# Write order of permuted copies, list lengths and a new pick string in an attention and Fourier-mixing kernel

## The chip, the core and the metric

The kernel runs on one core of a Trainium2 chip. A core has a matrix engine (TensorE, PE in the profile), a vector engine (VectorE, DVE), a scalar engine (ScalarE, ACT), a general engine (GpSimd, POOL) and a queue engine (SyncE, SP), which here issues nearly all transfers. Each engine works off its own queue in order, and engines wait for one another through semaphores. Matrix products and transposes land in PSUM, which has eight banks; the other engines copy the results to SBUF, the working memory. The metric is the device time of one launch in microseconds (us).

## The reference

What is computed, cut to what matters (B = 8, H = 8, S = 576, D = 64, 128 features, model width 512, hidden width 2048, all float32):

```
def phi(x):                        # x = q or k, times 1/sqrt(sqrt(D))
    h = x @ omega.T - sum(x*x)/2
    h = h - max(h, axis=-1)
    return exp(h) / sqrt(128)
q_p, k_p = phi(q), phi(k)
kv  = einsum('bhsm,bhsd->bhmd', k_p, v);   z = sum(k_p, axis=2)
x   = (q_p @ kv) / (q_p @ z + 1e-6)        # heads joined: (B, S, 512)
u   = x + real(fft(fft(x, axis=1), axis=2))
un  = layernorm(u)
out = u + relu(un @ w_ch1) @ w_ch2
```

## The kernel before

The program has two parts, and each is written out from a list. A step (`Step`) names its engine (or two engines to choose from), an assumed length in us, the buffers and PSUM banks that it takes and gives back, and the events that it waits for. `Listing.run` takes one step after another from many streams and emits its instructions; the position in the list is the position in the engine's queue. In the second part, the step that could begin first by the assumed lengths and biases comes next. In the first part, a string `PICKS` (line 63) says for every step which stream goes on and, with a capital letter, that the second-best engine takes it. There the assumed lengths no longer choose the stream, but they still set which of two engines counts as the best, and which bank is taken.

**First part.** Three interleaved streams work through the 32 head pairs (8 batches, 4 pairs each). For one pair (`attn`):

- `loads` and `load_v` issue k, q (tile `kq`, two buffers) and v (`vd`) on SP.
- PE transposes the nine k and q blocks (line 511), ACT copies them out (`kqT`, L521).
- PE projects them on omega (L595), DVE takes the maxima (`nmx`, L539), ACT the exponentials (`e`, L556).
- PE forms kv (L629), and DVE or ACT copies it (`keep`, L643 or L645).
- PE transposes the nine query feature blocks (line 511) in three groups of 1, 4 and 4 blocks (j0 = 0, 1, 5). ACT copies each group from PSUM to `qeT`, permuting the tokens (`evicted`, L530), with two instructions for each group, one for each half of the tokens.
- PE multiplies with kv (L676, L684), DVE forms the reciprocal (L693, L694), and DVE or ACT scales the result to `x` (L705 or L701).

When a batch has its four pairs, `mix` does the Fourier transform: folds on DVE and POOL (L732 to L768), products (L788 to L849), copies (L811, L882), sums (L887 to L900); the rows go to DRAM (`us`, L914, L869, L925). Beside this, `weights` loads 32 blocks of the feed-forward weights as 64-bit floats (`raw`, L468) and `narrow` turns them into float32 on ACT, POOL and DVE (L436 to L454). `plain` runs the feed-forward network for the first 512 rows (L1034, L1057). `norm_of` (line 955) normalises 128 rows: statistics on DVE (L964 to L966), a power on POOL (L968), scaling on DVE (L970), transposes on PE (L974), a copy on ACT (L978).

**Second part.** The remaining 4096 rows go through the feed-forward network in eight blocks of 512 (L1241 and L1421 are its products), with `norm_of` for the next block woven in (`late_norms`). It has no pick string. `norm_of` gets its tile pool as an argument: `mlpp` in the first part, `late` in the second.

In `evicted`, the destination of a group is permuted over (h, s, t, c): c is the block inside the group, and h, t and s split the 128 tokens of a block. c is the fastest in memory. A group of four blocks (h = 4, s = 2, t = 16, c = 4) with j0 = 5 is written with t innermost, in steps of four elements (16 bytes). With j0 = 1 the same shape is written with c innermost, in memory order. The group with j0 = 0 has a single block (c = 1).

Of the kernel before, what the change touches and what calls it, by code (L numbers as in the profile page):

```python
# [14 lines left out]
AF = mybir.ActivationFunctionType  # L15
# [20 lines left out]
PE, ACT, DVE, POOL, SP, NONE = "pe", "act", "dve", "pool", "sp", "none"  # L36
# [3 lines left out]
class Clock(NamedTuple):  # L40
# [20 lines left out]


PICKS = (
    "ff40d00d3cacfgdbgce3gbbcecccegc8cbabfhg0iiii8ef9a89h827edhOiicfhedidjhggciee7ebhJhceadafaedafffbbffb"
    "bfacdceadjccjbhceecfbQcdbd877gjiih7ai7a77gcahKb8b8hgg79h8ehgjeecScjgicejddhhh8b9dgbgbjahdeddaffefcaj"
    "dcgbfgadhidgcf77hb7fefOI7hh1hg96ghif7ge7fQffhdfhfefgch77h8gddTbbjjHe8jfjj8d6k6ddkejmeegjiidhjhfgbhhd"
    "jefjifajkdljajggggNlkfkk7ajjhkdagieLML76m6lknjaa9aecnogaoooe8en8dlllm9cddJcbjj87ccQd9jhljiiildkhgmki"
    "ilghjhjhkfjThfgiQhjikgkhfiie7abj9il07j64758i85j56ijThilgf5dmbdkkegef6hggdc5hcbjibggakdmgbjeaj8l5k9am"
    "3da9hddRah7hjkak4j7j6dlihjfklmcd7jhhjfbef6Ijcemkkkjm6hjh7jgqkgmUdclD9icRicdemielhjjildmchj9milgjFoc9"
    "687nabdeke8ckbHWK7ffgjdi8cjdThfgfhfcklb4aclbjOjaaacca48iahf5Tacfdijefa759bbfbcg8g7aa7feg9b54Q67fdfie"  # L70
    "ggehe5lcdekRRfhccfhjiifkIeecjfickTdeegegebhh86efja9ajffkSagh5eghd9efg9fbddh9cjghjccdkicKccdbfdfhcKeK"
    "f9efdcbdhRc565fifih8fdM9L675SicjRiPPheh7hbhfdj5ggihiIfchfeajgohhdLeN756g8ik7jiibcaJicTajgihji96ha8fj"
    "dkgh7efieh4dch5caafejcdfh5cice9heeeghhbjcgggghlgmkjkcljdioablhmka8aiGI444ompdjh9dmd77ikc9mhngnjjjljk"
    "knminilmkimklknlllTioQJGfgihkagee8h7Whlmkl79h3ld7rlil98cbeg9Lnp9rqqln9mpnabq9dg8s6ejfqk8dYlg8WShcnom"
    "piddpgjijlpkpEfkpeppedphphcncom5mlebkjmjle76646dl5dRecbkimg36mm488kncmiMdMNi5L4fflek966clcdgndkRgei8"
    "gaiaUhjgeklkmml4immb0U0k8k9fjjfjhd2g6ki8m4ljagebdc9agb2hbcfihgddgge9ahPcchdaRhcQhhi8cjcecgLGff6fd9Qa"
    "88a2f7bf8g9R998gb9aM7b9ddbdd35472759eaef9bbfbbcbce9abec666f6g87hd8M7bdcLb6HfgcOKc24f9f79c888Qd8a8e48"
    "eb6bghdeeeca7c877cdcb54e8d4788Jcb4cccfe5ge9I9dKb9b8ec8dded8aadMfe1geg97e59g375f6hdaF8OidNeiahhdbi2hh"
    "cc4hfifjhgfgfihg2gR4ehcS4fjj8gUcaeifcjjggj4bg8ddMf52i46ghhaacb65caKdNdNb3643a891442a6792364755bb76bF"
    "9a8bbb8accd4857bd87d7MaccbLDbbEaL9ccIa249c9a9dbc27eeN9ce8O765e588af73ab979de876aee1fcgdi9SichSa5a5f5"  # L80
    "5e145446cc9GM5ccabc7JaI553958888359012964432bcdb56Nb78b78daca58c78a7187676c56978b0e6510G1bF8a9a77486"
    "75992847bD6F333a77909K929aaFFF5CC66566666622241021110"
)


# [195 lines left out]
def kernel(  # L281
# [10 lines left out]
    nc = tc.nc  # L292
# [54 lines left out]
    mlpp = early.enter_context(tc.tile_pool(name="mlp", bufs=2))  # L347
# [7 lines left out]
    def psum_of(b):  # L355

        i = b.ids[0]
        return banks[:, i] if len(b.ids) == 1 else banks[:, i : i + 2]

    def got():  # L360

        return listing.got, psum_of(listing.got)
# [150 lines left out]
        return dst  # L513

    def evicted(dst, b, j0, j1, makes, order):
        cost = 0.01 + 0.222 * (j1 - j0) if order else 0.05 + 0.107 * (j1 - j0)
        yield Step(ACT, cost, 0.02, makes=makes + (j0,), give=(b,), bias=0.08)
        ps = psum_of(b)[:, 0 : 128 * (j1 - j0)].rearrange("q (c p) -> q c p", p=128)
        dst = dst[:, j0:j1, :]
        if order is None:  # L520
            nc.scalar.activation(out=dst, in_=ps, func=AF.Copy)  # L521
            return
        h, s, t = order[j0]
        dst = dst.rearrange("q c p -> q (c p)").rearrange("q (h s t c) -> q s c h t", h=h, s=s, t=t)
        ps = ps.rearrange("q c (h t s) -> q s c h t", h=h, s=s)
        for i in range(s):
            of, to = ps[:, i, ::-1, :, ::-1] if i and j0 else ps[:, i], dst[:, i]
            if j0 == 1:
                of, to = (a.rearrange("q c h t -> q h t c") for a in (of, to))
            nc.scalar.activation(out=to, in_=of, func=AF.Copy)  # L530

    def softmax(n, ts, num, b, es):

# [183 lines left out]
    def mix(b):  # L717
# [7 lines left out]
        def folds(n):  # L725
            op = (ALU.add, ALU.subtract)[n]
            even, odd = (ALU.subtract, ALU.add) if n else (ALU.add, ALU.subtract)
            step = Step({DVE: 1.135, POOL: 2.45}, take=("half",), port=True)
            yield step
            eng = nc.gpsimd if step.eng == POOL else nc.vector  # L730
            h = fft.tile([P, NC3 + 1, DM], F32, name="half", tag="half")
            eng.tensor_tensor(out=h[:, 0:NL], in0=x[:, 0:NL], in1=x[:, NL : 2 * NL], op=op)  # L732
            yield Step(DVE, 1.0, port=True, bias=-0.08)
            nc.vector.tensor_copy(
                out=h[:, NL, 0 : 2 * QD + 1 : 2 * QD], in_=x[:, 4, 0 : 2 * QD + 1 : 2 * QD]
            )
            for dst, src in ((h[:, 0:NL], h[:, 0:NL]), (h[:, NL : NL + 1], x[:, 4:5])):
                nc.vector.tensor_tensor(
                    out=dst[:, :, 1 : 2 * QD],
                    in0=src[:, :, 1 : 2 * QD],  # L740
                    in1=src[:, :, DM - 1 : 2 * QD : -1],
                    op=op,
                )
            step = Step({DVE: 0.91, POOL: 1.55}, port=True)
            yield step
            eng = nc.gpsimd if step.eng == POOL else nc.vector
            for dst, o in ((NC3, ALU.add), (1, ALU.subtract)):
                eng.tensor_tensor(
                    out=h[:, dst, 0 : 2 * QD + 1],
                    in0=h[:, 0, 0 : 2 * QD + 1],  # L750
                    in1=h[:, 1, 0 : 2 * QD + 1],
                    op=o,
                )
            step = Step(
                {DVE: 1.2, POOL: 2.2},
                makes=("fold", b, n), give=("half",), port=True, bias=-1.41,
            )
            yield step
            eng = nc.gpsimd if step.eng == POOL else nc.vector
            for m, o in ((0, even), (1, odd)):  # L760
                eng.tensor_tensor(
                    out=fold[:, :, 2 * n + m, :],
                    in0=h[:, 1 : NC3 + 1, 0:QD],
                    in1=h[:, 1 : NC3 + 1, 2 * QD : QD : -1],
                    op=o,
                )
            middle = fold[:, :, 3, 0:1] if n else mid_t[:]
            eng.tensor_copy(out=middle, in_=h[:, 1 : NC3 + 1, QD : QD + 1])  # L768
# [5 lines left out]
        for n, (tab, name) in enumerate(((cs, "cs"), (sn, "sn"))):  # L774
# [4 lines left out]
                take=("duo",) + (("y",) if n == 0 else ()),  # L779
# [40 lines left out]
        for c in range(NC3):  # L820
# [6 lines left out]
                take=("duo",),  # L827
# [30 lines left out]
            order = ((1, 0), (1, 1), (0, 0), (0, 1)) if c < NL else ((1, 0), (0, 0), (1, 1), (0, 1))  # L858
# [77 lines left out]
    def load_rows(dst, t):  # L936
        nc.sync.dma_start(dst, us[P * t : P * (t + 1), :])
# [17 lines left out]
    def norm_of(j, t, i, pool, dst):  # L955

        yield Step(SP, 0.42, 3.0, take=("u",), kb=256)
        u = pool.tile([P, DM], F32, name="u", tag="u", bufs=2)
        load_rows(u[:], t)
        st = small.tile([P, 6], F32, name="st", tag="st")  # L960
        mv = small.tile([P, 2], F32, name="mv", tag="mv")
        rstd = small.tile([P, 1], F32, name="rstd", tag="rstd")
        yield Step(DVE, 1.12, bias=-0.23)
        nc.vector.bn_stats(out=st[:], in_=u[:])  # L964
        nc.vector.bn_aggr(out=mv[:], in_=st[:])
        nc.vector.tensor_scalar(rstd[:], mv[:, 1:2], 1e-6, None, op0=ALU.add)  # L966
        yield Step(POOL, 1.05, port=True, bias=-0.18)
        nc.gpsimd.tensor_tensor(rstd[:], rstd[:], mhalf[:], op=ALU.pow)  # L968
        yield Step(DVE, 0.455, port=True)
        nc.vector.tensor_scalar(u[:], u[:], mv[:, 0:1], rstd[:], op0=ALU.subtract, op1=ALU.mult)  # L970
        yield Step(PE, 0.437, take=("bank",), give=("u",))
        b, tp = got()
        for dc in range(NDC):
            nc.tensor.transpose(  # L974
                tp[:, 128 * dc : 128 * dc + 128], u[:, 128 * dc : 128 * dc + 128], ident[:]
            )
        yield Step(ACT, 0.5, give=(b,), makes=("unT", j, i), bias=0.33)
        nc.scalar.activation(  # L978
            out=dst,
            in_=tp.rearrange("p (d t) -> p d t", d=NDC),  # L980
            func=AF.Copy,
        )
# [576 lines left out]
```

## Time and profile before

| | us |
|---|---|
| median of 3 runs (lowest, highest) | 1189.73 (1189.64, 1195.36) |
| the profiled execution | 1192.05 |
| its span, first to last instruction | 1190.2 |
| first product of the second part | 428.6 |

| engine | busy us | share of the span | instructions |
|---|---|---|---|
| PE (matmul) | 1166.4 | 98% | 12765 |
| DVE | 689.0 | 58% | 1482 |
| ACT | 484.1 | 41% | 1602 |
| POOL | 457.2 | 38% | 506 |

The chain of work that ended last, followed back from the last instruction, lies 87% on PE, 4% on ACT, 4% on DVE and 2% on DMA. Rows of the groups that the change names:

| line, engine | what | count | mean ns |
|---|---|---|---|
| L530 ACT | `qeT` from PSUM, 128x256 | 128 | 599 |
| L530 ACT | `qeT` from PSUM, 128x64 | 64 | 314 |
| L732 POOL | `half` from x, 128x1024 | 9 | 2368 |
| L732 DVE | `half` from x, 128x1024 | 7 | 1237 |
| L964, L965, L966 DVE | statistics | 36 each | 684, 182, 154 |
| L968 POOL | the power | 36 | 832 |

A mean over instructions that follow each other closely counts their overlap twice: the time that such an instruction holds its engine is read from one start to the next. Matmul rows overlap in the same way, and a matmul that waits for its operands inside its row counts as busy.

### The profile page before, as it was taken

The page shows a single profiled execution, that of the slowest core. Times are in us where ns is not written, and L with a number is a line of the kernel's source. Part 1 is how long each engine was busy: PE and PEld are TensorE (multiplying, and loading weights), DVE is VectorE, ACT ScalarE, POOL GpSimd, SP SyncE. Part 2 cuts the span into 40 slices and gives each one's busy share as a digit, 9 for nine tenths or more (in the row PEclk, how much of TensorE's full clock was granted, in tenths as well). Part 3 has the DMA queues.
Part 4 walks back from the last instruction along what each step waited for, and adds up shares of the span by engine and source line. Part 5 has one row for each costly group of instructions (what it writes and reads, how often), then busy time and mean ns, then how long its engine had stood idle before and what let it go on. Part 6 is the DMA issues. An engine that isn't in the chain of part 4 may idle for free.

```text
span 1190.2 us, 31894 instructions
## 1 busy us (share of the span) xinstructions
PE 1166.4 (98%) x12765; PEld 1043.5 (88%) x12765; DVE 689.0 (58%) x1482; ACT 484.1 (41%) x1602; POOL 457.2 (38%) x506
## 2 busy tenths in 40 slices
PE   8899999999999999999999999999999999999998
PEld 7778788879787878998998998999999899899898
DVE  5889899986565541752562572464374275256245
ACT  7889899878555212222222222222222222222211
POOL 2455554355354324315314324333332431531521
PEclk9999999999999999999999999999999999999999
DMA  9656856566475260852672573384194185177255
GB/s 260 171 171 183 250 148 210 164 199 190 140 229 167 76 211 10 276 188 69 227 234 80 163 263 115 111 287 143 52 302 131 66 290 179 63 238 222 80 162 193
DMA packets 144708, 205.71 MB, mean 173 GB/s; under 512 B 49072, under 2 KB 58544, under 8 KB 144560
## 3 DMA queue, kind: packets, MB, share of 16 engines
q1 hardware_dynamic: 144064, 203.41, 54.2%
q8 instruction: 101, 1.65, 0.6%
q14 instruction: 47, 0.39, 0.1%
q10 hardware_dynamic: 496, 0.26, 0.1%
HBM read 171.90 MB, written 35.91 MB: 175 GB/s over the span
## 4 chain that ended last, share of the span: by engine, by line
PE 87%; ACT 4%; DVE 4%; DMA 2%; issue 1%; SPq 1%; POOL 0%; DVEq 0%; ACTq 0%; POOLq 0%
PE banks L1241 33%; PE banks L1421 29%; PE banks L1034 5%; PE banks L1057 4%; PE banks L595 4%; PE banks L511 4%; ACT e L556 3%; PE banks L629 2%; PE banks L676 2%; PE banks L838 1%; PE banks L788 1%; DMA kq<-in_q_dram 1%; PE banks L974 1%; DVE nmx L539 1%; DMA raw<-in_moe_w_ch_dram 1%
## 5 line engine op out<-in xcount | busy, mean ns | idle before, releaser
L1421 PE MATMUL banks<-wl,sums 128*128 128x128 f32 x1792 | 219.6, 275 | 0.4
L1421 PEld LDWEIGHTS banks<-wl,sums 128*128 128x128 f32 x1792 | 210.5, 192 | 2.2 <-issue 1.5
L1227 DVE CUSTOM_DVE_ANT_0 hid<-banks,s 128x256 f32<-128x256 f32 x192 | 78.4, 422 | 224.6 <-PE banks L1241 219.8
L1255 ACT ACTIVATE s<-banks 128x256 f32<-128x256 f32 x192 | 73.8, 384 | 247.3 <-PE banks L1241 243.9
L556 ACT ACTIVATE e<-banks,nmx 128x128 f32<-128x128 f32 x576 | 165.1, 447 | 17.8 <-DVE nmx L539 17.2
L1241 PE MATMUL banks<-unT,w 128*128 128x256 f32 x704 | 168.6, 379 | 0.0
L1241 PEld LDWEIGHTS banks<-unT,w 128*128 128x128 f32 x704 | 132.2, 190 | 17.5 <-issue 0.5
L1396 ACT ACTIVATE s<-banks 128x128 f32<-128x128 f32 x168 | 46.6, 278 | 247.1 <-PE banks L1421 192.5
L1401 DVE TENSOR_TENSOR part<-banks,s 128x128 f32<-128x128 f32 x168 | 48.7, 290 | 138.1 <-PE banks L1421 137.9
L1241 PE MATMUL banks<-tt,w1s 128*128 128x256 f32 x512 | 125.0, 379 | 0.0
L1308 POOL TENSOR_TENSOR hs<-hid 128x256 f32<-128x256 f32 x64 | 46.6, 728 | 192.3 <-DVE hid L1227 166.8
L1241 PEld LDWEIGHTS banks<-tt,w1s 128*128 128x128 f32 x512 | 97.2, 190 | 13.3
L539 DVE TENSOR_REDUCE nmx<-banks 128x8 f32<-128x1024 f32 (+1 forms) x96 | 89.3, 951 | 24.8 <-PE banks L595 22.3
L1421 PE MATMUL banks<-wl,hid 128*128 128x128 f32 x768 | 98.8, 275 | 0.0
L1421 PEld LDWEIGHTS banks<-wl,hid 128*128 128x128 f32 x768 | 94.0, 192 | 1.2
L595 PE MATMUL banks<-om,kqT 64*64 64x128 f32 x2304 | 79.1, 274 | 4.4 <-ACT kv L645 1.6
L1308 POOL TENSOR_TENSOR hs<-hid,hs 128x256 f32<-128x256 f32 x64 | 46.6, 728 | 90.2 <-issue 69.6
L1241 PE MATMUL banks<-unT,w1s 128*128 128x256 f32 x320 | 79.5, 379 | 0.0
L968 POOL TENSOR_TENSOR rstd<-rstd,mhalf 128x1 f32<-128x1 f32 x36 | 29.9, 832 | 128.7 <-DVE rstd L966 128.7
L595 PEld LDWEIGHTS banks<-om,kqT 64*64 64x64 f32 x2304 | 63.3, 133 | 15.2 <-issue 4.6
L1421 PE MATMUL banks<-wl,hs 128*128 128x128 f32 x576 | 74.2, 276 | 0.4 <-DVE part L1401 0.4
L530 ACT ACTIVATE qeT<-banks 128x256 f32<-128x256 f32 (+1 forms) x192 | 69.3, 504 | 7.2 <-PE banks L511 6.9
(128 smaller groups left out, 2002.1 us busy)
## 6 DMA issues: line engine op xcount, KB each, us to landing
wl<-w2l SPq DMA_DIRECT2D x392, 256.0 KB, 3.7
raw<-in_moe_w_ch_dram SPq DMA_DIRECT2D x32, 512.0 KB, 5.2
kq<-in_k_dram SPq DMA_DIRECT2D x32, 288.0 KB, 4.5
vd<-in_v_dram SPq DMA_DIRECT2D x32, 288.0 KB, 4.3
kq<-in_q_dram SPq DMA_DIRECT2D x32, 288.0 KB, 4.6
u<-us SPq DMA_DIRECT2D x36, 256.0 KB, 3.7
ur<-us SPq DMA_DIRECT2D x36, 256.0 KB, 4.0
out_dram<-ur SPq DMA_DIRECT2D x34, 256.0 KB, 2.4
```

The source lines that it names most:

```text
L511: nc.tensor.transpose(ps[:, (j - j0) * 128 : (j - j0 + 1) * 128], src(j), ident[:])
L530: nc.scalar.activation(out=to, in_=of, func=AF.Copy)
L539: nc.vector.tensor_reduce(nmx[:, :, 0:num], pps[:, :, 0 : MF * num].rearrange("p b (c m) -> p b c m", m=MF), axis=AX.X, op=ALU.max, negate ...
L556: nc.scalar.activation(out=e[:, c + (i if num == 1 else 0), :], in_=pps[:, i, MF * c : MF * c + MF], func=AF.Exp, bias=nmx[:, i, c : c + 1],)
L595: nc.tensor.matmul(pps[cols, c, MF * m : MF * m + MF], lhsT=kqT[rows, j, cols], rhs=om2[rows, :],)
L1034: nc.tensor.matmul(hp[:, 0:TP], lhsT=w1[:, dc, 128 * fc : 128 * fc + 128], rhs=unTs[key][:, dc, :], start=(dc == 0), stop=(dc == NDC - 1),)
L1227: nc.vector._custom_dve(TENSOR_ADD_SAT, out=o, in0=ps, in1=sb, s0=FMAX, s1=0.0)
L1241: nc.tensor.matmul(ps[:, 0:HT], lhsT=left(dc), rhs=right(dc), start=start and dc == 0, stop=(dc == D2 - 1), skip_group_check=True,)
L1255: nc.scalar.activation(out=s[:], in_=ps[:, 0:HT], func=AF.Copy)
L1308: nc.gpsimd.tensor_tensor(out=o, in0=l, in1=r, op=op)
L1401: nc.vector.tensor_tensor(out=part[:, t, 128 * m : 128 * m + 128], in0=ps[:, 0:128], in1=saved[with_][:], op=ALU.add,)
L1421: nc.tensor.matmul(ps[:, 0:128], lhsT=left[:, f], rhs=wls[j, i, n][:, f], start=start and f == 0, stop=(f == 3), skip_group_check=True,)
```

## The change

The copies of a group are written with c innermost for every group, not only for j0 = 1. The assumed length of such a copy pair changes from 0.01 + 0.222 m to 0.13 + 0.1 m for m blocks. The fold on POOL gets 2.75 for 2.45. The statistics and the power keep 1.12 and 1.05 in the first part and get 1.01 and 0.85 in the second. The pick string of the first part is another one of the same length, 1853 characters; it is said to come from a new search with later transfers.

```diff
 PICKS = (
-    "ff40d00d3cacfgdbgce3gbbcecccegc8cbabfhg0iiii8ef9a89h827edhOiicfhedidjhggciee7ebhJhceadafaedafffbbffb"
...
+    "40e0f03eafdaegebg3bdbbeefccdcccfce8affgg0hhig8ib2La887efjjgeeejjHhighifdjgijdlhhefTfkkefeifhbdfiefhi"
...
     def evicted(dst, b, j0, j1, makes, order):
-        cost = 0.01 + 0.222 * (j1 - j0) if order else 0.05 + 0.107 * (j1 - j0)
+        cost = (0.13 + 0.1 * (j1 - j0)) if order else 0.05 + 0.107 * (j1 - j0)
...
         h, s, t = order[j0]
-        dst = dst.rearrange("q c p -> q (c p)").rearrange("q (h s t c) -> q s c h t", h=h, s=s, t=t)
-        ps = ps.rearrange("q c (h t s) -> q s c h t", h=h, s=s)
+        dst = dst.rearrange("q c p -> q (c p)").rearrange("q (h s t c) -> q s h t c", h=h, s=s, t=t)
+        ps = ps.rearrange("q c (h t s) -> q s h t c", h=h, s=s)
         for i in range(s):
-            of, to = ps[:, i, ::-1, :, ::-1] if i and j0 else ps[:, i], dst[:, i]
-            if j0 == 1:
-                of, to = (a.rearrange("q c h t -> q h t c") for a in (of, to))
-            nc.scalar.activation(out=to, in_=of, func=AF.Copy)
+            of = ps[:, i, :, ::-1, ::-1] if i and j0 else ps[:, i]
+            nc.scalar.activation(out=dst[:, i], in_=of, func=AF.Copy)
...
-            step = Step({DVE: 1.135, POOL: 2.45}, take=("half",), port=True)
+            step = Step({DVE: 1.135, POOL: 2.75}, take=("half",), port=True)
...
-        yield Step(DVE, 1.12, bias=-0.23)
+        yield Step(DVE, 1.12 if pool is mlpp else 1.01, bias=-0.23)
...
-        yield Step(POOL, 1.05, port=True, bias=-0.18)
+        yield Step(POOL, 1.05 if pool is mlpp else 0.85, port=True, bias=-0.18)
```

More of the change, by code (lines that the diff above doesn't have):

```diff
@@ L63 @@
 PICKS = (
-    "ff40d00d3cacfgdbgce3gbbcecccegc8cbabfhg0iiii8ef9a89h827edhOiicfhedidjhggciee7ebhJhceadafaedafffbbffb"
[L65 to L82, printed above, removed]
+    "40e0f03eafdaegebg3bdbbeefccdcccfce8affgg0hhig8ib2La887efjjgeeejjHhighifdjgijdlhhefTfkkefeifhbdfiefhi"
+    "hfjgfkd9elelkjdheefdefQRLbce9h77gh7ijg8cbi877ggk7fihjmngeed87TdecedhIa7g9gg99ieeccdHcdggbhfcgfebbaci"
@@ new lines @@
+    "ebccebRfiedaeecf98g7fI7hh1hgg89g6gh8eecg96geaefehceaefg78hh7i9bk79jQ9ghjjf86k6ddkgjdldgiiidhfhcgfhhd"
+    "eifjhf6ldinliiIlghgjibmmmILfhflkfljafLLL77lkjmehcomL9pjjjdjOa9hj6a8hhibfegbgij87ddQe9jhljiimidkhgmkj"
+    "mjgiiilhkfjThfgiikj9jfmfigieiccb7ki9lll8j0k64c59kik5k86lhh7hge7h6ekie5if9ghccdfihddiifaedleeifM75fce"
+    "jkd8bjicj8f8imim9fa3j8iglmn9cjfmiib8kdigce7ikiknmkmbh4cpfdbDqSZllmnFFo5nkaf9bejkllj9ak7hhg9iUhigih8T"
+    "lmeIeeggkidlcm7mjdhhddbi77ibKckeiedb4ice8hb6hah8SceghihiMg5eghklfgiih9Ig7gg9b69hh9bKcbgbch54Q78higfi"
@@ new lines @@
+    "deeffg5ddfjcTcdigjeiedfgjhdmInmTjcgfedjhdbh67egkOa9khgkSa9hh5eghdf99bhgdegdacjgckeccgckhfhckdk9jJjij"
+    "JQec9agba8cLa75i5ggih6hdUdG6j8jjTPjgg9gk57f5hdieleigIdejeihdiijkiGgibeL7875g7jgh6U8a99mmijh8jfk8kgea"
+    "jf9di4gf6c5gei5ea9becjeeecghghbcjcdkfhgglfljkjh9giiackibhe5nebkkf9kJ55o4mkllQmifebek4jij557iikk9jjji"
+    "mikhjkkhkiikikjlinij5JnPfjNF7efdffcc78b5kjj8lk6bae6i95W98jg3fhRefm66nfikkehhkmlcccffifhihjj6nldmiimn"
+    "lmldofkhndamm48a47j4hf5khaaa8nkmm68mkj76lijknSk8iiJi9gknihne43lmccicjomaEONU76jh7mopkhjbinpijbhkkiIl"
@@ new lines @@
+    "5bh7jidl6klbSfihhagll50jT7eg7eikhjhh7gkhfikj0gcdcifdbiehijfmlcn2Ob5mm3k9acdc8h9g5h7eedhdgd77cbQd5gg2"
+    "e9e367e78hibbMG4bbb58ccK9dLa8cfea2fecKdebecdeccefbIPbcb9hdhM6k52gbbMg5bfP7NR987ac98NPb85e8de5e6c5ec9"
+    "ahagabc9dcecaeee5d8ababb9c899cKd9bedccde7fc98dgSghedggig18789bi6G45jjUi1e9gRc5863f4feL69afg3MRd8b4Eg"
+    "gdc6bbe4ddeehdheimfhbifamfgccebcddhidjgjedddeT47466g4PgQ4eff1a977bb3bb833aLJ579b395I99ab9e998dbab694"
+    "7c9dddgdf5hhhPfe9ead9cce7G9ed34438ge9FdHc9dcLd5ed98LcddbhheabedabddfhePdcfaafffI4daaJ9Mcce8beefd4cc2"
@@ L83 @@
+    "adeab27OOOM8a9K5659b0664dccdda7a2ccMccd40296cdeIP97ce8bcf6c8ddabac1aaI9d52bb9e661abec5D915G7bcd5Ed9C"
+    "5bHHa9983763a3b4399F5414335aaaaE499954423225530320210"
 )
```

## The prediction

> **What bounds the kernel now.** I read the execution first by stretch of time, then the chain of waits inside the stretches, then single instructions on ScalarE (ACT). In the table below each row is a stretch: busy time of TensorE's matmuls (PE), its weight loads (PEld), VectorE (DVE), ScalarE (ACT) and GpSimd (POOL), then the granted clock, the share of the DMA engines and GB/s.
>
> ```profile
> 10.00:150.00 140.00, 128.05 (x3056) 108.08 (x3048) 118.41 (x240) 121.11 (x425) 67.42 (x56) 0.99 0.70 206
> 150.00:250.00 100.00, 99.93 (x2071) 85.43 (x2065) 92.31 (x209) 89.89 (x321) 47.14 (x45) 1.00 0.61 180
> 250.00:428.60 178.60, 177.80 (x2546) 140.04 (x2545) 106.32 (x244) 97.19 (x347) 75.52 (x72) 1.00 0.51 157
> 428.60:1190.20 761.60, 753.18 (x5040) 703.97 (x5039) 370.31 (x788) 172.40 (x507) 266.25 (x323) 1.00 0.52 169
> ```
>
> The second part starts at 428.6 us and is TensorE almost throughout. So is the first part from 150 us on: its chain of waits there is almost only PE rows. Only in 10 to 150 us is TensorE starved. A busy PE row flatters it, since short matmuls wait inside their rows. Counting the matmuls of that stretch at the pace that each kind keeps inside an unbroken run (transposes at 0.11 us, 72 projections in 1.97 us, 72 of the kv product in 1.21 us, and so on) gives about 113 us of work in 140: some **27 us of headroom**. The same count gives 98 of 100 us after 150 and all of 178.6 after 250, so nothing to win there. In 10 to 150 us the chain changes hands between ACT (about 45 us), DVE, PE and DMA landings. ACT and DVE are both 85% busy.
>
> **The copies.** The change alters one group of three per head pair. The first group of one block has c = 1, so its two orders are the same one. The middle group (j0 = 1) is written in memory order already. Only the last group (j0 = 5) changes: 32 pairs of copies, 64 of 192 instructions. The trace holds the new form beside the old. In the timeline of ACT (start, length, instruction), first the three groups of one late head pair in their order (single block, middle group, last group), then a last group and a middle group, each with the instruction that follows it without a gap:
>
> ```profile
> 330.60 0.34 ACT L530 ACTIVATE qeT<-banks 128x64 f32<-128x64 f32 x2 [2.61 <-PE banks L511]
> 336.25 0.80 ACT L530 ACTIVATE qeT<-banks 128x256 f32<-128x256 f32 x2
> 338.73 1.13 ACT L530 ACTIVATE qeT<-banks 128x256 f32<-128x256 f32 x2
> ```
> ```profile
> 200.42 1.12 ACT L530 ACTIVATE qeT<-banks 128x256 f32<-128x256 f32 x2
> 201.31 0.65 ACT L521 ACTIVATE kqT<-banks 128x512 f32<-128x512 f32 x1
> ...
> 354.14 0.66 ACT L530 ACTIVATE qeT<-banks 128x256 f32<-128x256 f32 x2 [1.39 <-PE banks L511]
> 354.69 2.69 ACT L556 ACTIVATE e<-banks,nmx 128x128 f32<-128x128 f32 x10
> ```
>
> From one start to the next, the old form holds ACT for 201.31 - 200.42 = 0.89 us, the memory order for 354.69 - 354.14 = 0.55. Others give 0.88 to 0.91 and 0.53. Saved: 0.36 x 32 = **11.5 us of ACT**, of which 14 head pairs, 5.0 us, lie in 10 to 150 us.
>
> [...] The new order reads PSUM in hops of 512 bytes where the old one hopped 8. If that hop had a price, the sum would be nothing or a loss. But the middle group reads with just this hop and takes 0.53, so by the row I take 0.36. [...]
>
> How much of 5.0 us arrives at the end? The chain in the stretch runs over only two changed copies (54.2 and 68.5 us): 0.7 us at least. All of it would be 5.0. ACT has 45 of 140 us of the chain, a third: I take **-1.7 us**. After 150 us ACT's 6.5 us are covered by PE; if a new order uncovered it there, they would count too.
>
> **The new order of the first part.** Instructions and transfers keep their number, apart from choices between two engines. What changes is who stands ahead of whom on all five queues, SP's DMA issues among them. The strings show no more than that: both hold 1853 picks, with 126 and 129 choices of the other engine. So I bound it from the places where TensorE visibly waits. The dearest:
>
> ```profile
> 32.59 0.28 DVE L643 COPY kv<-banks 128x130 f32<-128x130 f32 x1
> ...
> 32.93 2.00 PE L676 MATMUL banks<-kv,qeT 128*64 128x65 f32 x32 [3.03 <-DVE kv L643]
> ```
> ```profile
> 32.00:33.00 1.00, 0.07 (x2) 0.08 (x4) 1.00 (x3) 0.41 (x3) 0.10 (x1) 0.78 0.11 40
> 33.00:34.00 1.00, 1.00 (x20) 1.00 (x22) 1.00 (x3) 1.00 (x6) 1.00 (x1) 0.50 0.00 0
> 34.00:35.00 1.00, 1.00 (x24) 1.00 (x22) 0.86 (x2) 1.00 (x6) 0.86 (x1) 0.50 0.41 111
> 35.00:36.00 1.00, 1.00 (x12) 0.88 (x9) 0.52 (x3) 0.60 (x4) 0.00 (x0) 0.52 0.83 233
> ```
>
> The kv copy stood on DVE behind a weight step and two maxima, PE waited 3.03 us, and then three microseconds ran at half clock: 1.5 us more. [...] Further waits: 0.32 us at 81 and 0.89 + 0.57 us at 142 to 144 for late q and k, 1.25 us at 85.4 where the row names no releaser, 0.72 us at 90.4 for ACT. Sum of the visible ones: 4.5 + 1.8 + 1.25 + 0.72 = 8.3 us. Late landings hold much of the chain too:
>
> ```profile
> 77.31 3.54 DMA kq<-in_q_dram
> ...
> 115.06 5.47 DMA raw<-in_moe_w_ch_dram
> ...
> 137.46 6.00 DMA kq<-in_q_dram
> ```
>
> If "later transfers" means that the search reckoned with later landings, these waits shrink. If weight loads move back, the 18 weight blocks converted before 150 us (about 44 us of DVE in rows L441 to L454) thin out and give DVE room, which the feed-forward work pays later. A new order removes some of these waits and makes others. The ends: the 8.3 us gone with a few more, -12, or two new gaps of the dear kind, +9. I take a little over a third of the visible: **-3 us**. The longer POOL length (2.75 for 2.45) removes no instruction; the row of the POOL fold has 2.36 us median, and the reserve only makes the order wait for POOL with more margin. Cost: nothing, and within the above if wrong.
>
> **The second part.** Its order is chosen by due times, and two lengths fall: statistics 1.12 to 1.01 (rows 0.684 + 0.182 + 0.154 = 1.02) and the power 1.05 to 0.85 (row 0.83). No instruction gets faster; the list believes each normalised block ready 0.31 us sooner. PE's waits name exactly this chain:
>
> ```profile
> PE banks L974 <- DVE u L970: 3.5, 7, 0.5
> ```
>
> Once in each of seven blocks, L970 stands on DVE behind a sum that takes 1.27 us beside a POOL addition. If L970 is listed ahead of that sum: -3.5. If the transposes go one product earlier (0.895 us) on PE and L970 stays: 7 x 0.9 = +6. Nearest to the row is that the place barely moves: I take **-0.5**. Nothing else on PE waits there, so a moved DVE or POOL step has cover of microseconds.
>
> **Sum.** -1.7 - 3 - 0.5 = -5.2 us. The profiled execution took 1192.05 us (span 1190.2, 1.85 around it), 2.3 above the median of 1189.73; the differences are differences of span, so they are set against the median: 1189.7 - 5.2 = **1184.5 us**.
>
> **Rivals.** *The early stretch opens up*: all 5.0 us of ACT count, and the visible 8.3 us go: 1189.7 - 13.3, about 1176.5. For it: 27 us of headroom; against: DVE is as full as ACT and gets nothing from the copies. Chance 0.22. *Hidden*: DVE takes over as the bound, the order wins and loses alike: only 0.7 us, 1189. For it: DVE has 118 of 140 us busy. Chance 0.20. *Starved by the queue of transfers* (the slower side): SP issues all loads of both kinds in one queue; q, k and weights land 4.5 to 5.2 us after issue in the median. A k or q load put behind weight loads some 3 us later opens a PE gap of 3 us, which costs 4.5 with the half clock. One such place is paid by the rest; from the second on the kernel is slower: 1189.7 - 1.7 + 9 = 1197. Against it: only 1.8 us of such waits now. Chance 0.20. *That the change does less than it says* is certain in part (32 of 96 copies) and counted.
>
> **Numbers.** Forecast 0.38, rivals 0.22, 0.20, 0.20. About 0.5% (6 us) is what a measurement of this kernel can tell from no change; that is 1183.8. Half of the forecast's case lies below it (0.19), with the first rival 0.41. The other half, the hidden case and 0.02 of the last one give 0.41. Slower: 0.18. Forecast's own range 1179 to 1189; the range that leaves out 2 in 10: 1174 to 1196.
>
> **What would show it.** All L530 pairs of 256 at 0.53 us from start to start, and the group's mean near 0.45 us (0.599 now) with 128 instructions. The end of the first part (428.6) earlier by 4 to 5 us. No half clock between 30 and 36 us. Less ACT in the chain before 150 us. The L970 wait per block shorter or gone. Wrong if the long copies stay at 0.89, if the first part ends at 428 or later although ACT is 11 us lighter, or if PE rows after 10 us show gaps of over 3 us with a kq or vd landing behind them.

## The result, and the profile after

| | before | after |
|---|---|---|
| median, us (lowest to highest, 16 runs each) | 1190.36 (1187.1 to 1195.36) | 1186.95 (1183.67 to 1189.98) |
| profiled execution, us | 1192.05 | 1187.5 |
| its span | 1190.2 | 1185.6 |
| first product of the second part | 428.4 | 428.3 |
| second part, from there to the end of the span | 761.8 | 757.3 |
| ACT busy | 484.1 | 470.1 |

The ratio is 0.9969 with a 95% interval of 0.9956 to 0.9982: 3.4 to 3.7 us gained. That is less than the 0.5% that the prediction took as the least which can be told from no change, but the interval leaves 1 out. The forecast was 1184.5.

(Line numbers of the changed kernel are lower by 2 than those before: L528 is L530, L674 is L676, L968 is L970, L1239 is L1241.) The first product of the second part stands at 428.4 us in the trace before; the 428.6 of the table further up is a little late. The two rows of the parts already say most: the first part ends where it ended, and the whole gain lies in the second. Two lines of the groups by source carry these times: the products of the second part, with the time of the first and of the last one.

```profile
L1241 PE MATMUL banks<-unT,w x704: 379/379/382, 428.4 to 1141.2; 128*128 128x256 f32 x176
```
```profile
L1239 PE MATMUL banks<-unT,w x704: 379/379/382, 428.3 to 1136.7; 128*128 128x256 f32 x176
```

From first to last product it was 712.8 us before and is 708.4 now. Two of the stretches of the prediction, after the change (columns as there):

```profile
10.00:150.00 140.00, 128.15 (x3055) 110.01 (x3048) 117.60 (x239) 118.87 (x434) 61.25 (x54) 0.98 0.70 207
...
428.60:1185.60 757.00, 752.15 (x5040) 702.86 (x5038) 381.69 (x802) 169.85 (x507) 238.29 (x309) 1.00 0.52 171
```

TensorE does the same number of matmuls in 10 to 150 us (3055 for 3056), in the same time. In the last row its idle time falls from 761.60 - 753.18 = 8.42 us to 757.00 - 752.15 = 4.85, and its busy time by 1.0. The idle part is one wait, `L974 <- DVE u L970` (3.5 us in 7 blocks), which is no longer in the list of waits. The timeline of one block shows why, first before, then after:

```profile
604.77 1.27 POOL L1461 TENSOR_TENSOR ur<-ur,part 128x512 f32<-128x512 f32 x1 [2.45 <-ACT part L1454]
...
605.31 1.27 DVE L1388 TENSOR_TENSOR sums<-hid,sums 128x512 f32<-128x512 f32 x1 [0.44 <-PE banks L1421]
...
606.51 0.53 DVE L970 TENSOR_SCALAR u<-u,mv,rstd 128x512 f32<-128x512 f32 x1
...
607.10 0.66 PE L974 MATMUL banks<-ident,u 128*128 128x128 f32 x4 [0.50 <-DVE u L970]
```
```profile
604.72 0.99 DVE L968 TENSOR_SCALAR u<-u,mv,rstd 128x512 f32<-128x512 f32 x2
...
605.31 1.11 PE L972 MATMUL banks<-ident,u 128*128 128x128 f32 x8
...
607.35 0.69 DVE L1386 TENSOR_TENSOR sums<-hid,sums 128x512 f32<-128x512 f32 x1 [0.44 <-PE banks L1419]
```

Before, the last scaling of the block stood on DVE behind a sum of 1.27 us, and PE waited for it. Now the list has two scalings run together ahead of that sum, and PE transposes both in one row of eight. The sum comes later, where nothing waits for it, and takes 0.69 us: no POOL addition runs beside it any more.

The order is not all that moved. The additions of the results (L1461, after L1459) may go to POOL or to DVE, and in the second part the list chooses the engine by the assumed lengths too. The larger of the two groups on POOL, before and after:

```profile
L1461 POOL TENSOR_TENSOR ur<-ur,part x31: 1267/1269/1729, 492.5 to 1182.9; 128x512 f32<-128x512 f32 x31
```
```profile
L1459 POOL TENSOR_TENSOR ur<-ur,part x24: 1266/1267/1338, 492.4 to 1178.3; 128x512 f32<-128x512 f32 x24
```

With the smaller group (8 before, 1 after), 39 of the 87 additions were on POOL and 25 are now. In the block above this alone would do: a sum of 0.69 instead of 1.27 us would end 0.58 us sooner, and PE waited 0.50 us (an estimate from these rows). Which of the two, the place of the scaling or the engine of the addition, brings how much was not separated.

The copies became what they were to become. ACT in the timeline, a group of four blocks and the copy behind it, and the totals of all such groups (busy us, mean ns):

```profile
200.42 0.66 ACT L528 ACTIVATE qeT<-banks 128x256 f32<-128x256 f32 x2
200.96 0.28 ACT L521 ACTIVATE kqT<-banks 128x128 f32<-128x128 f32 x1
```
```profile
L528 ACT ACTIVATE qeT<-banks 128x256 f32<-128x256 f32 x128 | 43.8, 455 | 10.0 <-PE banks L511 9.5
```

0.54 us from start to start where the changed group had 0.89, a mean of 455 ns over all 128 instructions where it was 599, and ACT is 14 us less busy (11.5 of them were counted from the copies). Yet the first part is not shorter. TensorE's longest waits there were 3.0 us for `kv` and then some of about 1 us. The list of them after begins so (us in all, times, the longest):

```profile
PE banks L674 <- issue: 4.6, 1, 4.6
PE banks L511 <- DMA kq<-in_q_dram: 2.0, 2, 1.6
```

The kv wait is gone, and a longer one, with no releaser that the trace names ("issue"), has come. It lies at 20 to 25 us, in the middle of one product, and the half clock that used to come at 33 to 36 us follows it:

```profile
19.70 0.56 PE L674 MATMUL banks<-kv,qeT 128*64 128x65 f32 x11
...
24.84 1.36 PE L674 MATMUL banks<-kv,qeT 128*64 128x65 f32 x21 [4.57 <-issue]
```
```profile
23.00:24.00 1.00, 0.00 (x0) 0.00 (x0) 0.00 (x0) 0.00 (x0) 0.33 (x1) 0.53 1.25 237
25.00:26.00 1.00, 1.00 (x23) 1.00 (x24) 0.00 (x0) 0.00 (x0) 0.00 (x0) 0.50 0.47 98
```

Eleven of the product's 32 matmuls run, then PE stands, and 21 run. In the first window row DVE and ACT stand too, since they wait for PE (6.34 us until L682, 4.87 us until L511). The clock (the third number from the end) is down to a half at 23 us, and is still there in the busy microsecond from 25 us on; it comes back at 29.9.

### The profile page after: what moved, and what is told of

Its sections match the earlier page's. It is cut to its first block, busy times and chain, and to the rows that moved or that the text cites. A ratio compares the mean times of both kernels' runs of the same rounds, so it can differ in the third digit from the quotient of the medians.

```text
span 1185.6 us, 31878 instructions
## 1 busy us (share of the span) xinstructions
PE 1165.1 (98%) x12765; PEld 1044.6 (88%) x12765; DVE 697.8 (59%) x1488; ACT 470.1 (40%) x1597; POOL 417.6 (35%) x496
## 3 DMA queue, kind: packets, MB, share of 16 engines
q8 instruction: 101, 1.65, 0.6%
## 4 chain that ended last, share of the span: by engine, by line
PE 92%; ACT 2%; DVE 2%; DMA 2%; issue 1%; SPq 1%; POOL 0%; DVEq 0%; ACTq 0%
PE banks L1239 33%; PE banks L1419 30%; PE banks L1055 5%; PE banks L1032 5%; PE banks L511 5%; PE banks L593 4%; PE banks L627 3%; PE banks L674 2%; PE banks L972 2%; PE banks L836 1%; ACT e L554 1%; PE banks L786 1%; PE banks L796 1%; DMA kq<-in_q_dram 1%; PE banks L847 1%
## 5 line engine op out<-in xcount | busy, mean ns | idle before, releaser
L1239 PE MATMUL banks<-unT,w 128*128 128x256 f32 x704 | 167.5, 379 | 0.0
L1239 PEld LDWEIGHTS banks<-unT,w 128*128 128x128 f32 x704 | 132.7, 190 | 17.9 <-issue 0.5
L1239 PE MATMUL banks<-tt,w1s 128*128 128x256 f32 x512 | 126.2, 379 | 0.0
L1239 PEld LDWEIGHTS banks<-tt,w1s 128*128 128x128 f32 x512 | 97.2, 190 | 13.3
L1239 PE MATMUL banks<-unT,w1s 128*128 128x256 f32 x320 | 80.7, 379 | 0.0
L966 POOL TENSOR_TENSOR rstd<-rstd,mhalf 128x1 f32<-128x1 f32 x36 | 24.1, 668 | 146.1 <-DVE rstd L964 145.1
L1419 PEld LDWEIGHTS banks<-wl,hs 128*128 128x128 f32 x576 | 70.0, 192 | 0.9 <-DVE part L1399 0.6
```

What stands on the lines that cost most here:

```text
L1239: nc.tensor.matmul(ps[:, 0:HT], lhsT=left(dc), rhs=right(dc), start=start and dc == 0, stop=(dc == D2 - 1), skip_group_check=True,)
L1419: nc.tensor.matmul(ps[:, 0:128], lhsT=left[:, f], rhs=wls[j, i, n][:, f], start=start and f == 0, stop=(f == 3), skip_group_check=True,)
```

## The experiments

The theories were these. *Lengths*: the whole gain is the second part's new order, made by the two lengths. *Copies and picks*: the lighter ACT, or the new order of the first part, brings part of it. Then, formed from the trace after: *late instructions*: the gap in L674 is no wait for data, but the next block of PE's own instructions arriving late behind the transfers, and it gives back what the new order won.

Two measures are used. The ratio to the kernel before has the interval of its runs. The length of the second part comes from the profiled execution; it repeats within 0.3 us wherever the order is the same, while the end of the first part lies between 424.3 and 430.2 us over all profiles, and at 425.7 and 429.3 in two of one and the same kernel. One profile's first part therefore proves nothing of a few us; for it, the median less the second part less 1.85 us around the span is used ("first part by the median"): 427.0 for the kernel before, over 88 runs (median 1190.7).

### One part of the change alone

**The two lengths alone**, on the kernel before:

```diff
-        yield Step(DVE, 1.12, bias=-0.23)
+        yield Step(DVE, 1.12 if pool is mlpp else 1.01, bias=-0.23)
...
-        yield Step(POOL, 1.05, port=True, bias=-0.18)
+        yield Step(POOL, 1.05 if pool is mlpp else 0.85, port=True, bias=-0.18)
```

> The kernel before with nothing but the two lengths of the second part (1.01 and 0.85). Theory 1 (the gain is the second part's): from the start of the second part to the end 757.0 us as in the changed kernel (761.6 before), no wait of the transposes L974 for L970, the time 3.5 to 4.5 us below the kernel before. Theory 2 (the gain is the first part's, as most of the forecast had it): 0.5 us below, at most 1.

Measured: 1186.21 us, ratio 0.9951 (0.9937 to 0.9966). Second part 1185.8 - 428.6 = 757.2. The lengths alone give everything that the whole change gives.

**The write order alone**, with the old picks and lengths, so that every engine's order stays as before:

```diff
-        dst = dst.rearrange("q c p -> q (c p)").rearrange("q (h s t c) -> q s c h t", h=h, s=s, t=t)
+        dst = dst.rearrange("q c p -> q (c p)").rearrange("q (h s t c) -> q s h t c", h=h, s=s, t=t)
...
```

> The kernel before with nothing but the write order of the last group; assumed lengths, picks and so the order on every engine as before. The last groups take 0.53 us from start to start instead of 0.89 (ACT 11 us less busy). Theory 1: the end of the first part stays within 1 us of 428.6, the time within 1 us of before. Theory 2: 1.7 us less (0.7 to 5.0).

Measured: 1191.76 us, ratio 1.0002 (0.9991 to 1.0013), second part 761.8. Shorter copies alone, in the same order, give nothing: the interval reaches to a gain of 1.1 us, less than the 1.7 that the prediction took.

**The changed kernel without the two lengths** (1.12 and 1.05 everywhere):

> The changed kernel with 1.12 and 1.05 in the second part also. Theory 1 (the gain is the second part's): as the kernel before within 1 us, the second part 761.6 us long, the waits of L974 for L970 back (3.5 us). Theory 2: 0.5 us above the changed kernel.

Measured: 1190.06 us, ratio 0.9997 (0.9983 to 1.0011), second part 1186.5 - 424.8 = 761.7. Copies, new picks and POOL's 2.75 together are worth nothing that can be told. With the lengths alone, this closes the sum from both sides.

**The power's length alone**, on the kernel before (0.85 for 1.05 in the second part):

> The kernel before with only the power's length changed in the second part (0.85), statistics at 1.12. If this length alone lets L970 and the transposes find their place: as e1 within 1 us, no waits of L974. If it needs both: part of the 3.5 us of waits stays, 1 to 3 us below the kernel before.

Measured: 1195.49 us, ratio 1.0041 (1.0026 to 1.0057), second part 1192.5 - 426.8 = 765.7. Neither expectation came true: half of the edit loses 4 us where the whole one wins 4.5. PE's waits in the second part name a wait that neither whole kernel has at this size:

```profile
PE banks L1421 <- DVE part L1401: 2.7, 7, 0.4
PE banks L1421 <- issue: 1.5, 5, 0.3
```

PE's wait for L970 is gone here too, and yet the time is longer, so the loss takes another way than the gain; the chain of waits still runs over a scaling in one block (L970, 0.55 us at 612.45). The additions went the other way as well:

```profile
L1461 POOL TENSOR_TENSOR ur<-ur,part x45: 1263/1268/1720, 490.9 to 1185.3; 128x512 f32<-128x512 f32 x45
```

With 8 of the smaller group, 53 additions are on POOL, and more sums of DVE are long: the timeline shows 31 that begin beside a sum on POOL and take over 1 us, against 24 before and 10 after the whole change (there 7 more take 0.997 or 0.998 us). In all the runs compared here the second part is the longer, the more additions POOL has: 757.2 to 757.3 us with 25 (both lengths alone, the whole change), 761.7 to 761.8 with 39 (before, the write order alone, the change without the lengths), 765.7 with 53. That is a correlation; no run fixed the engine of the additions. What is shown is that a length acts as a sorting key, of places and of engines, and that its size doesn't tell which way the time goes.

### The first part

**The changed kernel again**, to see what repeats:

> The changed kernel once more, as the mark for the others, and a second profile of it. Time 3.4 us below the kernel before. If the gap of 4.57 us in TensorE's queue near 20 us belongs to this order, it stands in this profile too, in the same instructions; if it was an accident of one execution, it is gone and the first part ends some 5 us before 428.

Measured: 1187.07 us, ratio 0.9951 (0.9939 to 0.9963). The gap is back, after the same eleventh matmul:

```profile
20.12 0.56 PE L674 MATMUL banks<-kv,qeT 128*64 128x65 f32 x11
25.58 1.35 PE L674 MATMUL banks<-kv,qeT 128*64 128x65 f32 x21 [4.89 <-issue]
```

**Write order and lengths with the old picks**, on two occasions:

> The kernel before with the write order and the second part's lengths, but the old picks of the first part. Theory 1: as fast as e1 within 1 us, and at least as fast as the changed kernel, because the new picks bring nothing. Theory 2: about 2 us below the kernel before and some 3 us slower than the changed kernel, which has the new picks besides.

> e3 once more, to tell it from the changed kernel. If the new picks bring nothing or cost something: 0.5 to 0.7% below the kernel before, so at least as fast as the changed kernel (0.3 to 0.5% below). If e3 was luck: 0.3 to 0.5% like the changed kernel and e1.

Measured: 1184.57 us, ratio 0.9934 (0.9921 to 0.9947), then 1186.37 us, 0.9957 (0.9941 to 0.9972). The first seemed to say that the old picks were better than the new ones; the second doesn't. One kernel, two intervals that hardly overlap: from one occasion to another, differences of 0.2% between variants can't be told. Old and new picks are not shown to differ.

**The changed kernel with the old write order**:

> The changed kernel with the old write order of the last group (0.89 us a pair), its order on every engine unchanged. If the new order, searched with the short copies, leans on them: slower than the changed kernel by 2 to 5 us, most of it before 150 us. If they are hidden in this order as they were in the old one (e2): within 1 us.

Measured: 1188.22 us, ratio 0.9977 (0.9966 to 0.9988), second part 757.4. Against the 0.9969 of the changed kernel that is 1 us worse, inside the intervals. The gap is there too (4.1 us), so the copies don't make it.

**Transfers held back.** The changed kernel, with the transfers of two Fourier tables (`cs`, `sn`), of v of the fourth and fifth head pair, or of both, issued only behind the table `cd`; the list's order of all else stays:

```diff
+            if n == "cd":
+                while held:
+                    held.pop(0)()
...
-                nc.sync.dma_start(tab_sb[n][p0:p1], src[p0:p1])
+                put_off(n in ('cs', 'sn'), lambda n=n, src=src, p0=p0, p1=p1: nc.sync.dma_start(tab_sb[n][p0:p1], src[p0:p1]))
```

> The changed kernel, with six transfers of the early stretch (four of the tables cs and sn, and v of head pairs 3 and 4) issued on SP only when the table cd is issued, at about 25 us instead of 12 to 22; nothing else moves. Theory 3 (the gap of 4.6 to 4.9 us in TensorE's queue inside the products L674 is a block of its own instructions arriving late behind these transfers): the gap is gone or under 1 us, the half clock after it too, the first part ends 4 to 7 us earlier, the time is 4 to 7 us below the changed kernel. Theory 4 (the gap is part of this order of instructions, whatever the transfers do): gap and time stay within 1 us of the changed kernel, or it is slower, because v arrives late.

> As e5, but only the two transfers of v wait for cd. Theory 3: part of e5's effect, since the tables still stand in front of the instruction block: a gap between 1 and 4 us, the time 1 to 4 us below the changed kernel. Theory 4: as the changed kernel.

> As e5, but only the four transfers of the tables cs and sn wait for cd, the two of v stay. Theory 3 (instruction block behind the transfers): e6 kept its gap of 4.6 us, so the tables carry most of e5's effect: gap under 1 us, first part as short as e5's within 2 us. If tables and v are both needed: a gap of 1 to 4 us stays.

| held | median, us | ratio | gap in the product of L674, us | first part by the median |
|---|---|---|---|---|
| nothing (after; again) | 1186.95; 1187.07 | 0.9969; 0.9951 | 4.57; 4.89 | 427.8; 427.9 |
| both | 1184.26 | 0.9951 (0.9934 to 0.9967) | 0.29 | 425.1 |
| v | 1185.7 | 0.9966 (0.9953 to 0.9979) | 4.6 | 426.6 |
| tables | 1185.42 | 0.9944 (0.9926 to 0.9961) | 0.55 | 426.3 |

With both held, the same eleven and 21 matmuls (the line is L686 there):

```profile
21.59 0.56 PE L686 MATMUL banks<-kv,qeT 128*64 128x65 f32 x11
22.45 0.81 PE L686 MATMUL banks<-kv,qeT 128*64 128x65 f32 x21 [0.29 <-issue]
```

No data that this product reads was touched, and the gap went from 4.6 us to 0.3. Only the traffic ahead changed, and the tables alone make the difference: with only v held, the gap stayed at 4.6 us where 1 to 4 were expected. The time, though, fell by 2.7 us with both held, where 4 to 7 were expected. The DMA view of the kernel after, for 18 to 26 us, shows what was under way (queue, packets, MB, share of the 16 engines):

```profile
q1 hardware_dynamic: 3763, 1.90, 98.4%
q8 instruction: 1, 0.02, 0.8%
```

One packet of instructions (16 KB: over the whole run 101 such packets carry 1.65 MB) moves among 3763 packets of data that take 98.4% of the 16 DMA engines. It is seen at 22 to 23 us, and PE goes on at 24.84; in the repetition it is seen at 23 to 24 and PE goes on at 25.58; with both held it is seen at 20 to 22, and PE stops for 0.29 us only. By the rows the place costs 4.6 and 4.9 us in the two profiles of the changed kernel, and in the first of them about 2 us more for the 5.0 us of work behind it at half clock (an estimate: the same 21 matmuls took 1.36 us at half clock and 0.81 at full).

The trace doesn't say which engine the packet is for; PE's own count points to PE. PE has a shorter pause without a releaser at 15.78 us (0.91 us). From there to 24.84 us its rows hold 127 matmuls and 127 weight loads, 254 instructions; in the repetition, in the change without the lengths and with the tables held the two pauses are also 127 and 127 apart. From 24.84 us to the next such pause, at 99.53 us (0.23 us), it is 1650 and 1649, within 3 of 13 times 254. So the pauses lie 254 of PE's recorded instructions, or, within 3, a multiple of that, apart. Over the whole run PE has 12765 matmuls and 12765 weight loads, which is 100.5 times 254, and the packets of instructions are 101. That such a packet holds PE's next instructions, and that PE paused until it had come, is the author's estimate from these numbers; no run shows it directly.

But the place doesn't stay won. In the profile with the tables held, the pause 254 instructions earlier, in the product that had 0.91 and 0.69 us in the two profiles of the changed kernel, is 2.0 us long, and the half clock follows it (17 to 20 us):

```profile
16.53 1.92 PE L604 MATMUL banks<-om,kqT 64*64 64x128 f32 x30 [2.00 <-issue]
```

In the profile with both held, half clock comes from 9.3 to 12.8 us, with a wait of 2.3 us for k; that wait is not made by the holding, for the changed kernel has it too (1.54 and 2.61 us, both without half clock). The medians of the two are lower than those of the changed kernel by 1.5 to 2.8 us, but the intervals of the ratios overlap. No variant is shown to beat the changed kernel.

**The dear kv wait of the kernel before, taken away by itself.** Write order and lengths with the old picks, and the copy that PE waited 3.03 us for put on ACT:

```diff
-            if step.eng == DVE:
+            if step.eng == DVE and n != 2:
```

> The kernel of e3 (old picks, new write order, new lengths in the second part) with one copy moved: kv of the third head pair goes through ACT instead of DVE, where it stood behind a weight step and two maxima while TensorE waited 2.4 us and then ran at half clock for 3 us. If that visible wait is worth what the prediction put on it: wait and half clock gone, the first part 3 to 4.5 us shorter than in e3, the time near 1181. If the headroom there is taken by the next wait: less than 1 us.

Measured: 1187.65 us, ratio 0.9965 (0.9949 to 0.998); without this edit 0.9934 and 0.9957. The wait fell to 0.18 us, and no gain shows. The timeline behind it:

```profile
30.55 0.92 PE L676 MATMUL banks<-kv,qeT 128*64 128x65 f32 x24 [0.18 <-ACT kv L645]
32.62 0.45 PE L676 MATMUL banks<-kv,qeT 128*64 128x65 f32 x8 [1.15 <-issue]
...
34.83 1.41 PE L511 MATMUL banks<-ident,e 128*128 128x128 f32 x8 [1.26 <-ACT e L556]
```

PE comes 2.4 us earlier to the next two things that it lacks, 1.15 us without a releaser and 1.26 us for the exponentials, and then runs at half clock at 35 to 39 us all the same. So the visible wait was not a price; what it held back came to wait at the next two places.

## Why the prediction was right in the total and wrong in its steps

The sum said -5.2 us; -3.4 was measured, inside the forecast's own range. That the total came near is luck: it was reached by other terms than those that the prediction added up.

| step | taken | measured | by |
|---|---|---|---|
| copies, at the end of the run | -1.7 | 0 (-1.1 to +1.5) | the write order alone |
| new order of the first part | -3 | about 0, together with the copies | the change without the lengths |
| lengths of the second part | -0.5 | -4.5 (761.8 to 757.3) | the lengths alone, and the change without them |

**The copies** were read rightly as an operation: 0.55 us from the row of the middle group, 0.54 measured. If the hop of 512 bytes in PSUM has a price, the 0.35 us saved are what was left after it; no run changed the read without the write. What failed is the step "ACT has 45 of 140 us of the chain, a third". A share of the chain says where the chain passed, not what a shorter instruction on it brings. The rival *hidden* was right here in its size, whether or not DVE took over as it says; the 0.7 us of its two copies on the chain lie within what was measured.

**The new order** was priced by the visible waits, 8.3 us, "a little over a third" of it. The waits named went: the kv wait, the late q and k of 142 to 144 us (one of 1.6 us for q at 125 us came for them). From 30 to 150 us TensorE does 2711 matmuls now, 2539 before. But from 10 to 30 us it does 346 where it did 517, so that at 150 us the two are level (3055 and 3056). The rival *starved by the queue of transfers* had named the place and the price: one gap of the dear kind, paid by the rest of the gains. It had the wrong victim, though. The prediction looked for a kq or vd landing behind the gap; the gap's row names no landing, and the counts point to a packet of instructions, which is not shown directly. The 1.25 us at 85.4 us "where the row names no releaser" have the same signs (a packet of instructions at 84 to 85 us, data on 96 to 99% of the DMA engines; with the power's length alone, where this pause has 0.47 us, it lies 1397 matmuls and 1398 weight loads behind an earlier one, within 1 of 11 times 254), and were added to what could be won instead of being asked what they were. And the kv experiment shows that the price of 4.5 us for that wait was not to be won in the old order by this one edit.

**The lengths** were the mis-sized term. The prediction saw the right wait and the right end ("if L970 is listed ahead of that sum: -3.5"), and that is what happened, with 1.0 us less of busy rows on PE besides. What it did not ask is whether the lengths move the additions between POOL and DVE, which they did. Its other end was +6, and a loss of that order exists: the power's length alone gave +3.9, though no wait for L970 shows there, and that it came by the transposes is not shown. "Nearest to the row is that the place barely moves" was the failing choice. A list that picks the step that could begin first has no small moves at a tie: the instruction goes ahead of the sum or it doesn't, the addition goes to one engine or the other. Between ends so far apart a middle was no safe choice, and the list itself, which is deterministic, could have been followed by hand for one block: statistics, power and scaling end 0.31 us sooner, and one compares that with the due time of the sum that they compete with.

**The signs listed.** The pairs at 0.53 us, a mean near 0.45, no half clock at 30 to 36 us, less ACT in the chain of 10 to 150 us (28 us after, 45 before) and the L970 wait gone: all seen. The lighter chain on ACT made no shorter first part. The end of the first part 4 to 5 us earlier: not seen (428.3), which the prediction had named as the sign of being wrong, rightly for these two steps.

**Open.** Whether holding the tables back wins 1.5 to 2.8 us: its medians say so, the intervals don't. How often the gap of 4.6 us is there in executions without a profile; the five profiles that repeat it are all there is. Whether PE waited at 20 to 25 us for the packet of instructions, and if so, whether the tables' transfers delay it by the engines or by the queue. How much of the 4.5 us of the second part is the place of the scaling, and how much the 14 additions that left POOL. The statistics' length alone was not run.

## What to carry to other kernels

In a list that is ordered by assumed lengths, a length is a sorting key: test it as such, all lengths that meet at a tie together, and look at who is moved past whom, and to which engine, rather than at the size of the correction. Price the removal of a wait by what stands next behind it; a wait that is seen in a starved stretch can be only the place where slack shows. And separate the stretches before judging: here one part of the kernel repeats to 0.3 us and shows 4.5 us beyond doubt, while the other varies by up to 6 and can only be judged by medians.

## What the hardware showed that was not expected

- **A pause of PE without a releaser hung on the transfers ahead of it.** PE paused for 4.1 to 4.9 us (2.8 in a fifth profile) in the middle of one product, at the same instruction in all five profiles with this order and with the tables not held back. In the profile of the changed kernel the data queue took 98.4% of the 16 DMA engines from 18 to 26 us. With the tables held back the pause was 0.3 to 0.55 us. Such pauses lay 254 recorded PE instructions, or 11 or 13 times that within 3, apart. That PE lacked its own next instructions there is an estimate from these counts.
- **No length of a single wait told whether the half clock came.** It came with waits of 2.3 us (for k, with both held) and 2.0 us (with the tables held) and lasted some 3 us in each; the prediction's one case was 3.03 us. But behind a wait of 2.61 us for k, in the repetition of the changed kernel, the clock stayed at full. And with the kv copy on ACT it came at 35 us behind no wait of over 1.3 us, after four microseconds in which PE was busy for 17 to 57% of the time.
- **The two forms of a permuted copy differ by two thirds.** A 128x256 copy pair on ScalarE that writes in steps of 16 bytes and reads PSUM in hops of 8 takes 0.89 us; one that writes in memory order and reads in hops of 512 bytes takes 0.54. So what the contiguous write saves is more than what the longer hop may cost.
- **A VectorE sum took longer beside one on POOL.** Of the 128x512 sums and additions on VectorE in the second part of the kernel before that the timeline shows singly, 24 began while a sum ran on POOL, and each of them took 1.02 us or more; the other 234 took 0.69 at most.
